# One written-out program order for all engines in a fused attention and MLP kernel, with the MLP weights loaded ahead of the second group

## Chip, cores, metric

The kernel runs on one core of a Trainium2 chip. The metric is device time in microseconds, the median of several executions. A "profile" below is one execution taken by the hardware profiler; its span runs from the first to the last instruction and is about 1.8 us shorter than the time of the same execution. Each execution lists the mean granted TensorE clock, and is called slow when it is over 1.5% above the fastest of the same kernel.

## The reference

```python
# q, k, v: (4, 8, 768, 64); lam: (8,); blocks of 64 positions
intra = einsum('bhic,bhjc->bhij', qb, kb) * Dmask            # lower triangle, lam ** distance
intra = einsum('bhij,bhjd->bhid', intra, vb)
inter = einsum('bhid,bhde->bhie', qb * lam_pow, kv_state)
out[block] = intra + inter
kv_state = lam ** 64 * kv_state + einsum('bhsd,bhse->bhde', kb * rev_pow, vb)
# then an MLP on the 3072 tokens, d_model 512, d_ff 2048
h = x @ w_in
g = h + sin(alpha * h) ** 2 / alpha
y = g @ w_out
```

Attention is cut into 24 *units* (half of the heads, 256 positions of one batch). Four units make one *group* of 512 tokens, so there are six groups. For each group the MLP has 16 *first-layer blocks* (four matmuls of 512 columns each, then sine on ScalarE, square on some engine, and a VectorE step) and four output tiles of 16 second-layer matmuls, taken in *second-layer blocks* of four.

## The kernel before

The program order is the order of execution of each engine. The old program writes it with loops: attention for groups 0 and 1 first (eight units, with filler matmuls that keep the TensorE clock up), then the first layer of group 0, and from group 2 on a regular pattern in which one attention unit stands between eight MLP blocks.

```python
def group(g, tag):                      # units 0 to 7
    for n in range(n0, n0 + 4):
        ...                             # scale q and k of unit n + 1
        if n >= WIN0 and n < WIN0 + WCH:
            load_w_in(n - WIN0)         # WIN0 = 5
        okv = new_okv()
        if n > 0:
            intermm(n - 1, okv); outmm(n - 1, okv)
        scores(n); domask(n); kvmm(n, okv); kv_copy(n, okv); kv_decay(n, 0)
        ...
        if nxt:
            transposes(n + 1, tag, True)
        busy(NB)                        # NB = 4 filler matmuls

def slot(n, out=True):                  # units 8 to 23: one row on TensorE
    okv = new_okv()                     # one PSUM tile for outputs of n - 1 and k*v of n
    if out: intermm(n - 1, okv)
    if n < NU: scores(n)
    if out: outmm(n - 1, okv)
    if n < NU: kvmm(n, okv)
    ...                                 # copies, masks, kv update

for n in range(12, NU + 8):             # the steady part
    at = {0: [L(slot, n), ...], 1: [L(dec, ...), L(scale_k, n + 2, G), L(cast_v, n + 2, G)]}
    macro(at, "21212121" if n % 4 == 0 else ... "12121212")   # 1: first layer, 2: second layer
```

Squares in the steady part are on VectorE, scalings, v casts and kv updates on POOL, PSUM copies on ScalarE.

## Time and profile before

227.76 us median of 3 runs (226.99 to 228.04). The page of the old kernel: busy time of engines, then forty slices of the span, 5.7 us each; a digit is the busy share in tenths, and for PEclk the granted clock.

```profile
span 227.1 us, 5244 instructions
...
PE 207.8 (91%) x2054; PEld 108.9 (48%) x2077; DVE 158.3 (70%) x268; ACT 115.7 (51%) x200; POOL 114.0 (50%) x176
...
PE   8777679997997779999999999999999999999993
...
PEclk9996999999999969999999999999999999999999
DMA  5999599999769999984877777484233022201424
```

TensorE is the limit from about 85 us on (slice 15, counted from 0). Before that, slices with 6 and 7 show it waiting. Its timeline (start, duration, engine, source line, operation, output and inputs, form, count, and in brackets the idle time before and what ended it) shows the first MLP matmuls at 33.23 us (three records of this group are missing, so the true first one can lie 0.2 us earlier):

```profile
32.66 0.42 PE L320 MATMUL okv<-ST,VB 64*64 64x128 bf16 x16
33.23 2.97 PE L349 MATMUL hps<-xt,w_in_sb 128*128 128x512 bf16 x13 [0.16 <-issue]
```

In the steady part a unit is one row of matmuls between two MLP blocks. The same timeline around 101 us:

```profile
100.57 1.03 PE L377 MATMUL ops<-w_out_sb,gall 128*128 128x512 bf16 x4
101.43 0.22 PE L305 MATMUL okv<-QT,kvbd_1801 128*128 128x128 bf16 x1
...
101.75 0.42 PE L226 MATMUL sp<-QT 64*64 64x128 bf16 x16
102.00 0.39 PE L320 MATMUL okv<-ST,VB 64*64 64x128 bf16 x16
102.22 0.29 PE L254 MATMUL okv<-VB,KD 64*64 64x64 bf16 x16
102.45 1.04 PE L349 MATMUL hps<-xt,w_in_sb 128*128 128x512 bf16 x3
```

The unit begins at 101.43 and the next MLP block at 102.45: about 1.0 us for it. Durations overlap, so starts are what one reads here.

**A ledger.** I price TensorE's useful work by its undisturbed durations in this trace (a four-matmul MLP block 0.865 us, transposes of one q or k 0.22, scores 0.25, outputs 0.25 and 0.075 for each matmul with a kv state, k*v 0.25 or, from unit 16 on, 0.125), and call *lost* the start of an instruction minus the work before it. The old kernel has lost about 22 us at its first MLP matmul. "At the first block of group 1" is read for it at the same amount of work (25.1 us), as its order differs: 48.1 us, so 23.0 lost. At the end of TensorE's work (222.9 us) it has lost 30.2; a tail of 4.2 us follows, to store the last tile. The ledger is good to about 0.3 us.

### The profile page before, as it was taken

The page shows a single profiled execution, that of the slowest core. Times are in us where ns is not written, and L with a number is a line of the kernel's source. Part 1 is how long each engine was busy: PE and PEld are TensorE (multiplying, and loading weights), DVE is VectorE, ACT ScalarE, POOL GpSimd, SP SyncE. Part 2 cuts the span into 40 slices and gives each one's busy share as a digit, 9 for nine tenths or more (in the row PEclk, how much of TensorE's full clock was granted, in tenths as well). Part 3 has the DMA queues.
Part 4 walks back from the last instruction along what each step waited for, and adds up shares of the span by engine and source line. Part 5 has one row for each costly group of instructions (what it writes and reads, how often), then busy time and mean ns, then how long its engine had stood idle before and what let it go on. Part 6 is the DMA issues. An engine that isn't in the chain of part 4 may idle for free.

```text
span 227.1 us, 5244 instructions
## 1 busy us (share of the span) xinstructions
PE 207.8 (91%) x2054; PEld 108.9 (48%) x2077; DVE 158.3 (70%) x268; ACT 115.7 (51%) x200; POOL 114.0 (50%) x176
## 2 busy tenths in 40 slices
PE   8777679997997779999999999999999999999993
PEld 5465444433444345554554555455455444444452
DVE  3866756988895486798887998867987747667000
ACT  2463659964645345645554554445455535554121
POOL 5665995275635459999999855742611000000000
PEclk9996999999999969999999999999999999999999
DMA  5999599999769999984877777484233022201424
GB/s 149 293 289 274 139 177 185 216 213 168 227 166 171 243 204 299 200 207 95 210 158 173 153 190 180 102 208 62 56 73 68 0 49 46 46 9 40 92 49 92
DMA packets 63849, 33.92 MB, mean 149 GB/s; under 512 B 19648, under 2 KB 60880, under 8 KB 63824
## 3 DMA queue, kind: packets, MB, share of 16 engines
q1 hardware_dynamic: 59488, 29.31, 56.7%
q0 software_dynamic: 4224, 4.19, 11.4%
q8 instruction: 16, 0.26, 0.5%
q10 hardware_dynamic: 112, 0.07, 0.1%
q14 instruction: 9, 0.07, 0.1%
HBM read 27.28 MB, written 6.29 MB: 148 GB/s over the span
## 4 chain that ended last, share of the span: by engine, by line
PE 67%; DMA 11%; SPq 6%; DVE 5%; POOL 4%; issue 2%; ACT 2%; ACTq 0%; POOLq 0%
PE ops L377 32%; PE hps L349 26%; DMA st_v<-in_v_dram 8%; SPq L80 5%; DMA st_k<-in_k_dram 3%; PE sp L226 2%; DVE gall L363 2%; PE okv L320 2%; PE okv L305 2%; POOL KD L169 2%; SPq L209 1%; PE okv L254 1%; DVE QL L160 1%; PE bz L427 1%; PE pt L196 1%
## 5 line engine op out<-in xcount | busy, mean ns | idle before, releaser
L349 PE MATMUL hps<-xt,w_in_sb 128*128 128x512 bf16 x370 | 94.3, 379 | 2.4 <-DVE gall L363 1.5
L377 PE MATMUL ops<-w_out_sb,gall 128*128 128x512 bf16 (+1 forms) x391 | 94.7, 372 | 1.1 <-issue 0.7
L377 PEld LDWEIGHTS <-gall 128*128 128x128 bf16 x400 | 38.7, 98 | 42.9 <-issue 0.5
L349 PEld LDWEIGHTS <-w_in_sb 128*128 128x128 bf16 x384 | 36.8, 98 | 45.8 <-issue 3.0
L169 POOL TENSOR_TENSOR KD<-st_k,R 128x512 bf16<-128x512 f32 x24 | 27.5, 1144 | 13.0 <-DMA st_k<-in_k_dram 8.9
L237 DVE TENSOR_TENSOR ST<-sp,mask 128x512 bf16<-128x512 f32 x48 | 30.8, 683 | 3.3 <-PE sp L226 3.1
L384 ACT COPY ob<-ops 128x512 f32<-128x512 f32 (+1 forms) x25 | 14.2, 569 | 16.3 <-PE ops L377 16.3
L331 ACT CAST xt<-okv 128x512 bf16<-128x512 f32 x24 | 14.1, 586 | 6.7 <-PE okv L254 5.8
L178 ACT CAST VB<-st_v 128x512 bf16<-128x512 f32 x14 | 8.7, 623 | 14.8 <-DMA st_v<-in_v_dram 14.8
L160 POOL TENSOR_TENSOR QL<-st_q,E 128x512 bf16<-128x512 f32 x12 | 12.8, 1070 | 0.0
L427 PE MATMUL bz<-zeros 128*128 128x256 bf16 x60 | 10.6, 332 | 1.1 <-DVE warm L94 1.1
L226 PE MATMUL sp<-QT 64*64 64x128 bf16 x384 | 10.4, 228 | 1.2 <-ACT QT L200 0.7
L160 DVE TENSOR_TENSOR QL<-st_q,E 128x512 bf16<-128x512 f32 x12 | 8.7, 728 | 2.2 <-DMA st_q<-in_q_dram 2.1
L320 PE MATMUL okv<-ST,VB 64*64 64x128 bf16 x384 | 10.2, 226 | 0.0
L226 PEld LDWEIGHTS <-QT 64*64 64x64 bf16 x384 | 6.8, 111 | 3.6 <-issue 0.9
L427 PEld LDWEIGHTS <-zeros 128*128 128x128 bf16 x60 | 6.7, 119 | 2.7 <-DVE warm L94 1.1
L254 PE MATMUL okv<-VB,KD 64*64 64x64 bf16 x320 | 7.4, 198 | 0.1
L320 PEld LDWEIGHTS <-VB 64*64 64x64 bf16 x384 | 7.0, 111 | 1.0 <-issue 0.2
L180 POOL CAST VB<-st_v 128x512 bf16<-128x512 f32 x10 | 6.8, 683 | 0.0
L200 ACT COPY QT<-pt 128x512 bf16<-128x512 bf16 x8 | 4.7, 590 | 3.8 <-issue 1.7
L254 PEld LDWEIGHTS <-KD 64*64 64x64 bf16 x320 | 6.2, 114 | 0.4 <-issue 0.2
L196 PE MATMUL pt<-iden,KD 128*128 128x128 bf16 x32 | 3.4, 232 | 2.9 <-POOL KD L169 2.8
(530 smaller groups left out, 303.7 us busy)
## 6 DMA issues: line engine op xcount, KB each, us to landing
st_q<-in_q_dram SPq DMA_DIRECT2D x24, 256.0 KB, 3.6
st_k<-in_k_dram SPq DMA_DIRECT2D x24, 256.0 KB, 4.1
st_v<-in_v_dram SPq DMA_DIRECT2D x24, 256.0 KB, 4.4
out_dram<-ob SPq DMA_DIRECT2D x46, 128.0 KB, 2.5
w_in_sb<-in_moe_w_in_dram POOLq DMA_DIRECT2D x4, 512.0 KB, 6.6
w_out_sb<-in_moe_w_out_dram POOLq DMA_DIRECT2D x4, 512.0 KB, 15.3
QT<-QL SPq DMA_TRANSPOSE x16, 3.4
QT<-KD SPq DMA_TRANSPOSE x16, 2.6
```

The source lines that it names most:

```text
L80: ld = nc.sync.dma_start(out=tl[:].rearrange("p h two e -> p h (two e)"), in_=src[b, hh * HH:(hh + 1) * HH, tp * W:(tp + 1) * W, :] .rearr ...
L160: eng.tensor_tensor(out=QL[:], in0=stage[u][0][:].rearrange("p h two e -> p two h e"), in1=E[:, :, hs].unsqueeze(3).to_broadcast([P, 2, HH ...
L169: eng.tensor_tensor(out=KD[:], in0=stage[u][1][:].rearrange("p h two e -> p two h e"), in1=R[:, :, hs].unsqueeze(3).to_broadcast([P, 2, HH ...
L226: nc.tensor.matmul(out=sp[hd][half[c], par, hp, :], lhsT=QT[half[hd], 1, par, hp, half[c]], rhs=QT[half[hd], 0, :, hp, half[c]], start=Tru ...
L237: nc.vector.tensor_tensor(out=ST[:, hd], in0=sp[hd][:], in1=mask[:].unsqueeze(2).to_broadcast([P, 2, 2, P]), op=ALU.mult)
L254: nc.tensor.matmul(out=okv[half[hd], c, 2 * P + hp * D:2 * P + (hp + 1) * D], lhsT=KD[half[c], par, h, :], rhs=VB[half[c], par, h, :], sta ...
L320: nc.tensor.matmul(out=okv[half[hd], c, hp * P:(hp + 1) * P], lhsT=VB[half[c], par, 2 * hp + hd, :], rhs=ST[half[c], hd, par, hp, :], star ...
L331: nc.scalar.copy(out=xt[g][:, 2 * hh:2 * hh + 2, bb, :, :].rearrange("p hp c i -> p c hp i"), in_=okv[:, :, 0:2 * P].rearrange("p c (hp i) ...
L349: f1mm[g, f] = nc.tensor.matmul(out=hps, lhsT=w_in_sb[:, c, f * P:(f + 1) * P], rhs=xt[g][:, c].rearrange("p b c i -> p (b c i)"), start=( ...
L377: f2mm[:] = [nc.tensor.matmul(out=ops[:], lhsT=gall[g][:, f, m * P:(m + 1) * P], rhs=w_out_sb[:, f, col], start=(f == 0), stop=(f == NFC - ...
L384: nc.scalar.copy(out=ob[:], in_=ops[:])
L427: nc.tensor.matmul(out=bz[:], lhsT=zeros[:, :P], rhs=zeros[:], start=True, stop=True)
```

## The change

The intent: one explicit order of all steps on all engines, found offline on a model of engines and queues. The MLP is to start after group 0's attention alone, with w_in loaded before most of group 1's attention and w_out during the first layers of groups 0 and 1, so that TensorE is useful earlier. The loops are replaced by a list; a token is step.unit:engine(:PSUM bank), as `k.15:T` for k*v of unit 15 on TensorE, `sqr.1.10:V` for a square on VectorE, `wi.2:G` for chunk 2 of w_in issued by POOL.

```diff
+ORDER = """
+ld.0.0:S ld.0.1:S sk.0:V sq.0:G tq.0:T:3 tk.0:T:0 ld.0.2:S ...
+tq.1:T:3 tcq.1:V tk.1:T:2 tq.2:T:1 tck.1:V s.1:T m.1.0:V m.1.1:V tq.3:T:0 cv.3:A tcq.2:A o.0:T
+tk.2:T:3 tck.2:A tk.3:T:2 a.1.0:V n.1.0:G s.2:T sq.4:V sk.4:V x.0.0:A o.1:T tck.3:V ...
+...
+sk.6:V f1.0.0:T tk.5:T:3 f1a.0.1:T:2 f1.0.1:T f1a.0.2:T:4 f1.0.2:T wi.1:G m.4.1:V n.1.1:G k.5:T
+sin.0.0:A sin.0.1:A sin.0.2:A sqr.0.0:V f1a.0.3:T:5 f1.0.3:T kc.5:A tck.5:V sqr.0.1:G wi.2:G cv.6:V
+k.6:T sqr.0.2:A sin.0.3:A tk.6:T:0 stt.0.0:V wi.3:G sq.7:V ...
+...                                  # steady part: the pieces of a unit stand apart
+m.13.1:V k.15:T f2.1.0.3:T a.13.0:V kc.15:A oc.1.0:A s.14:T o.13:T sq.16:G sin.2.10:A cv.16:A
+x.13.0:A f2.1.1.0:T:3 a.14.0:V m.14.0:V tdq.16:S st.0.1.0:S st.0.1.1:S sq.17:G sq.18:G tdq.17:S
+...
+"""
-    NB = 4
-    for u in range(8):
-        load(u)
+    NKV, NQL, NQT, NST = 5, 4, 4, 3          # a little more buffering
...
-    def slot(n, out=True):
-        okv = new_okv()
+    def kvmm(u, **_):
+        okv[u] = ps.tile([P, 2, 512], FP32, name="okv", tag="okv", bufs=1)   # and the same in outmm
...
+    for item in ORDER.split():
+        name, eng, *bank = item.split(":")
+        kind, *ix = name.split(".")
+        DO[kind](*map(int, ix), eng=ENG[eng], bank=int(bank[0]) if bank else None)
```

The first four blocks of groups 0 and 1 are split into two halves (`f1a` and `f1`), so that a group may begin when half of its attention is ready. The arithmetic is unchanged; the filler matmuls between units go.

## The prediction

> From about 84 us on TensorE is the limit: busy 9.8 to 10.0 in each stretch of ten us, and the chain of waits is an unbroken row of four-matmul blocks of 0.86 us. A full round there (eight blocks plus one attention unit) takes 7.93 us, so a unit costs 7.93 - 8x0.864 = 1.0 us. All TensorE work is then 768 MLP matmuls x 0.216 = 166 us, 24 units = 24 us, transposes of eight units about 3.6 us: 194 us. The last matmul ends near 223.2, the store 3.9 us later. So the 84 us before the steady state hold nearly all the lost time: the timeline has the first MLP matmul only at 33.2 us, when 11-12 us of real work are done (21-22 us lost), and from there to the end 190 us pass for 182.6 us of work (7.4 us lost: group 0 paced by ScalarE/VectorE, then the 14.7 us in the chain for the st_v load of unit 8 behind w_out, POOL scaling, and one clock dip at 80-84 us).
>
> What the change does. Arithmetic stays; 32 filler matmuls go. Work moves between engines: by operations times traced durations DVE stays near 158 us, ScalarE rises from 116 to about 128, POOL falls slightly to 111. None exceeds TensorE's 194. The MLP starts after four units instead of eight (7 us of TensorE work), and w_in goes ahead of the loads of group two.
>
> Where the new start falls. Loads move at about 290 GB/s in the trace's packet records, one of 256 KB per 0.9 us. POOL issues w_in chunk 0 after casting v of unit 4, about 17 us. The Trainium skill, "DMA: Bandwidth & Descriptors" (Queues, rings and completion order), says the engines round-robin between queues packet by packet; this trace agrees: while w_out and loads shared the engines, w_out wrote 143 GB/s (286 read) and the loads got 72. So a w_in chunk needs about 3.7 us, landing near 22.5, and the loads crawl. In TensorE's order the transpose of q of unit 6 stands before the first MLP matmul and waits for the 19th load and POOL's 1.1 us scaling: start about 24 us, against 33.2. If no gap followed, the end would be 24 - 7 + 194 + 4 = 215 us.
>
> Gaps expected: q of unit 7 is scaled by POOL behind w_in chunks 2 and 3, themselves behind a square: 2-3 us at about 28-32 us. Without fillers the clock halves at times before and at the MLP start (this trace already dips for 3.4 us at 18.8 despite them): about 1 us. Group 0 and 1 are ScalarE-limited (32 us against 28 on TensorE up to the first second-layer matmul), partly hidden: 1-2 us. In units 8 to 11 and group 2 POOL and DVE are as full as TensorE: about 1 us. Sum about 4 (to 9). Prediction 219 us, range 214 to 224.5; faster by over 2% 0.8, within 2% 0.17, slower 0.03.
>
> Right if: first MLP matmul at 22-26 us; no TensorE loss after about 85 us; same 3.9 us tail; second-layer start about 54-58 us; granted clock lower before 30 us; ScalarE busy about 128 us.
>
> Wrong if: one late landing stalls all engines' strict orders; loads starve behind w_in longer than 4 us a chunk; DVE squares beside POOL stretch (0.42 to 1.2 us now) and pace group 2; or the order hides even the early gaps (then below 215).

## The result

The changed kernel takes 242.2 us median of 4 runs (239.75 to 243.52) against 227.38 us (226.55 to 228.04) for the old one on the same chip. Ratios are the mean time of one kernel's fast runs over the mean of the other's fast runs of the same rounds, so not quite the ratio of the medians: 1.053, with a 95% interval of 1.043 to 1.063. It is slower; 219.0 was predicted.

Two of the four runs, the profiled one among them, are slow (243.5 us; the fast ones are 239.75 and 240.9). The profile of the changed kernel is therefore read for what happens where, and sizes are taken from the experiments, most of whose profiles are of fast runs.

The page after:

```profile
span 241.7 us, 5272 instructions
...
PE 216.5 (90%) x2049; PEld 112.1 (46%) x2077; DVE 166.2 (69%) x290; ACT 119.1 (49%) x207; POOL 110.3 (46%) x148
...
PE   8487599699959999998999997999999999999990
...
PEclk9955569799979999999999999999999999999998
DMA  5999979990898999984863994404811200305314
```

The start is earlier and the clock is at half from 11 to 35 us (this is what the Trainium skill, "TensorE: Matmul & The Clock Gate", Part 1, says of an idle TensorE: it falls to a 4/8 clock and needs sustained work to come back; the trace agrees in that PEclk reads 5 there). But PE is "9", not full, in the later slices too. What TensorE waited for, in total, times and longest (us):

```profile
PE hps L452 <- DMA w_in_sb<-in_moe_w_in_dram: 3.7, 2, 1.9
PE hps L452 <- DVE gall L486: 2.9, 1, 2.9
...
PE ops L495 <- DVE gall L486: 1.3, 1, 1.3
```

The two waits for w_in in TensorE's timeline are the first MLP matmul, and block 8 of group 0, which needs chunk 2:

```profile
29.14 1.89 PE L452 MATMUL hps<-xt,w_in_sb 128*128 128x256 bf16 x8 [1.90 <-DMA w_in_sb<-in_moe_w_in_dram]
...
44.72 1.54 PE L452 MATMUL hps<-xt,w_in_sb 128*128 128x512 bf16 x4 [1.82 <-DMA w_in_sb<-in_moe_w_in_dram]
```

POOL's timeline says why chunk 2 was late. Chunks 2 and 3 stand in POOL's order behind a square (the row with output s), which waited 7.54 us for ScalarE's sine, and that for the first MLP block:

```profile
24.21 0.80 POOL L253 DMA_DIRECT2D w_in_sb<-in_moe_w_in_dram  x1
25.79 0.62 POOL L405 TENSOR_TENSOR kvs<-kvx,LHP 128x128 f32<-128x128 f32 x1 [0.78 <-DVE kvx L393]
33.96 1.07 POOL L481 TENSOR_TENSOR s<-s 128x512 bf16<-128x512 bf16 x1 [7.54 <-ACT s L472]
34.98 1.54 POOL L253 DMA_DIRECT2D w_in_sb<-in_moe_w_in_dram  x2
```

The chunks were issued at 34.98 and chunk 2 was used at 44.72, over 9 us later; the median from issue to landing was 9.6 us, against 6.6 in the old kernel.

The wait of 2.9 us on VectorE, at 69.6 us, comes from one square there and from what POOL did meanwhile. VectorE, then POOL:

```profile
64.05 3.98 DVE L481 TENSOR_TENSOR s<-s 128x512 bf16<-128x512 bf16 x1
67.95 0.28 DVE L405 TENSOR_TENSOR kvs<-kvx,LHP 128x128 f32<-128x128 f32 x1
```

```profile
63.87 0.80 POOL L261 DMA_DIRECT2D w_out_sb<-in_moe_w_out_dram  x1
64.69 1.05 POOL L276 TENSOR_TENSOR KD<-st_k,R 128x512 bf16<-128x512 f32 x1
65.70 2.04 POOL L276 TENSOR_TENSOR QL<-st_q,E 128x512 bf16<-128x512 f32 x2
```

The square takes 0.42 us in the median of this trace, here 3.98, and ends at 68.03, just after POOL's row of three scalings (67.74). The Trainium skill, "SBUF — State Buffer", section "SBUF: two separate sides", says that a VectorE operation with two SBUF inputs and a POOL operation that reads SBUF share one port pair under an exclusive lock, and the loser blocks. The square is such an operation. Its recorded start, however, is 0.64 us before that of the first scaling, while POOL was issuing a chunk of w_out; why it didn't finish in that time, the trace doesn't show.

The steady part after, for the same stretch of a unit's pieces:

```profile
132.53 0.42 PE L344 MATMUL sp<-QT 64*64 64x128 bf16 x16
132.88 0.40 PE L420 MATMUL okv<-QT,kvbd 128*128 128x128 bf16 x4
133.20 0.42 PE L429 MATMUL okv<-ST,VB 64*64 64x128 bf16 x16
133.55 1.90 PE L452 MATMUL hps<-xt,w_in_sb 128*128 128x512 bf16 x7
...
138.84 0.31 PE L375 MATMUL okv<-VB,KD 64*64 64x64 bf16 x8
```

Scores and outputs alone took 133.55 - 132.53 = 1.02 us of TensorE, and k*v comes later, by itself. At the end, the stores. Old kernel (ACT copies of the two halves of the last tile, and the last store's issue), then the changed one:

```profile
223.28 0.37 ACT L384 COPY ob<-ops 128x256 f32<-128x256 f32 x1 [1.37 <-PE ops L377]
223.68 0.55 ACTq L389 DMA_DIRECT2D out_dram<-ob  x1
```

```profile
236.24 0.37 ACT L267 COPY ob<-ops 128x256 f32<-128x256 f32 x1 [1.33 <-PE ops L518]
236.64 0.56 ACTq L528 DMA_DIRECT2D out_dram<-ob  x1
236.79 0.53 SPq L528 DMA_DIRECT2D out_dram<-ob  x1
237.36 1.40 SPq L510 DMA_DIRECT2D out_dram<-ob  x2
```

In the changed kernel two stores of earlier tiles (L510) are issued last, up to 238.8 us. The tail, from TensorE's end to the span's end, is 5.7 us instead of 4.2.

The ledger, in us lost by stage (e2, e3, e11 are experiments told below; each column sums):

| stage | before | after (slow run) | e3 (fast run, front as after) | e2 | e11 |
|---|---|---|---|---|---|
| up to the first block of group 1 | 23.0 | 30.0 | 26.6 | 23.1 | 23.0 |
| from there to the last block of group 1 | 6.4 | 5.8 | 3.8 | 4.3 | 4.2 |
| from there to TensorE's end | 0.8 | 7.5 | 6.9 | 7.2 | 6.0 |
| lost in all | 30.2 | 43.3 | 37.3 | 34.6 | 33.2 |
| tail | 4.2 | 5.7 | 5.7 | 5.6 | 4.1 |

So after minus before in these profiles is 7.0 - 0.6 + 6.7 + 1.5 = 14.6 us, which is 241.7 - 227.1. The front's part is 3.6 us in e3, a fast run with the same front. At the first MLP matmul both kernels have lost about 22 us: the changed one starts four microseconds earlier, with four microseconds less work done. In the old kernel's own profile, about 2 us of the 6.4 fall into a stretch at half clock from 80 to 84 us (the 6 in its PEclk row).

### The profile page after: what moved, and what is told of

The parts are those of the page before. It is cut to its first block, busy times and chain, and to the rows that moved or that the text cites. A ratio compares the mean times of both kernels' runs of the same rounds, so it can differ in the third digit from the quotient of the medians.

```text
span 241.7 us, 5272 instructions
## 1 busy us (share of the span) xinstructions
PE 216.5 (90%) x2049; PEld 112.1 (46%) x2077; DVE 166.2 (69%) x290; ACT 119.1 (49%) x207; POOL 110.3 (46%) x148
## 4 chain that ended last, share of the span: by engine, by line
PE 65%; DVE 9%; DMA 7%; issue 6%; ACT 4%; SPq 4%; POOL 2%; ACTq 0%; POOLq 0%
PE ops L495 31%; PE hps L452 25%; SPq L243 4%; DMA w_in_sb<-in_moe_w_in_dram 4%; DMA st_k<-in_k_dram 3%; ACT s L472 2%; DVE gall L486 2%; PE sp L344 2%; DVE s L481 2%; PE okv L429 2%; PE okv L420 2%; PE okv L375 1%; PE ops L518 1%; DVE ST L354 1%; DVE kvbd L397 1%
## 5 line engine op out<-in xcount | busy, mean ns | idle before, releaser
L452 PE MATMUL hps<-xt,w_in_sb 128*128 128x512 bf16 (+1 forms) x403 | 94.4, 379 | 7.4 <-DMA w_in_sb<-in_moe_w_in_dram 3.7
L472 ACT ACTIVATE s<-hps,alpha_sb 128x512 bf16<-128x512 f32 x96 | 64.9, 688 | 59.5 <-PE hps L452 50.5
L495 PE MATMUL ops<-w_out_sb,gall 128*128 128x512 bf16 x353 | 84.7, 381 | 2.8 <-DVE gall L486 1.3
L486 DVE SCALAR_TENSOR_TENSOR gall<-s,r_sb,hps 128x512 bf16<-128x512 bf16 x96 | 69.6, 742 | 22.7 <-POOL s L481 12.4
L481 POOL TENSOR_TENSOR s<-s 128x512 bf16<-128x512 bf16 x25 | 26.3, 1054 | 81.5 <-ACT s L472 72.1
L495 PEld LDWEIGHTS <-gall 128*128 128x128 bf16 x368 | 34.9, 98 | 42.9 <-issue 2.4
L481 DVE TENSOR_TENSOR s<-s 128x512 bf16<-128x512 bf16 x33 | 20.5, 621 | 11.0 <-ACT s L472 10.9
L479 ACT ACTIVATE s<-s 128x512 bf16<-128x512 bf16 x38 | 23.6, 630 | 0.9 <-DVE gall L486 0.3
L276 POOL TENSOR_TENSOR QL<-st_q,E 128x512 bf16<-128x512 f32 x19 | 20.4, 1075 | 4.2 <-DMA st_q<-in_q_dram 3.8
L267 ACT COPY ob<-ops 128x512 f32<-128x512 f32 (+1 forms) x16 | 8.9, 557 | 24.8 <-PE ops L495 22.3
L267 ACT CAST xt<-okv 128x512 bf16<-128x512 f32 (+1 forms) x18 | 10.4, 577 | 14.1 <-PE okv L429 14.1
L397 DVE TENSOR_TENSOR kvbd<-kvx,LBD 128x256 bf16<-128x256 f32 x17 | 11.4, 669 | 0.6
```

The lines of the kernel that those rows point to most:

```text
L267: nc.scalar.copy(out=out, in_=in_)
L276: eng.tensor_tensor(out=t[:], in0=stage[u, j][:].rearrange("p h two e -> p two h e"), in1=tab[:, :, hh * HH:(hh + 1) * HH].unsqueeze(3).to ...
L452: mlp[0] = nc.tensor.matmul(out=hps[g, f][:].rearrange("p (b i) -> p b i", b=2)[:, bs] .rearrange("p b i -> p (b i)"), lhsT=w_in_sb[:, c, ...
L472: nc.scalar.activation(out=s1[g, f][:], in_=hps[g, f][:], func=ACTF.Sin, scale=alpha_sb[:, f:f + 1])
L479: nc.scalar.activation(out=s2[g, f][:], in_=x[:], func=ACTF.Square)
L481: eng.tensor_tensor(out=s2[g, f][:], in0=x[:], in1=x[:], op=ALU.mult)
```

## The experiments

Fifteen kernels ran; all gave correct outputs. The theories: **A**, the half clock after the fillers went; **B**, late w_in chunks; **C**, VectorE work starved beside POOL; **D**, the order of the steady part; **E**, the order of the last stores; **G**, the early order of units 0 to 3, which delays the start.

### e1: fillers put back

```diff
# in the changed kernel, after each transpose pair, k*v and output step ahead of the first MLP matmul
+        for _ in range(8):
+            nc.tensor.matmul(out=unused_columns, lhsT=zeros[:, :P], rhs=zeros[:, :P], start=True, stop=True)
```

> The changed kernel with 8 filler matmuls (128 columns each, into unused PSUM columns) after each transpose, k*v and output step that stands before the first MLP matmul; nothing else moves. Theory A (the lost fillers leave the TensorE clock at half from 11 to 35 us, and this slows the early chain and the first MLP blocks): clock near 1.0 from about 10 us on, first MLP matmul no later than 29 us, 5 to 8 us faster than the changed kernel (about 232 to 236). Rival B (the loss comes from late w_in chunks and from squares on DVE beside POOL, the cold clock is only a symptom of waiting): under 3 us gain, the waits at 44.7 us for w_in and at 69.6 us for DVE stay as long as now.

Measured: 237.3, 238.7 and 240.6 us in the fast runs, at a mean clock of 0.99, ratio 1.049. The gain on the changed kernel's 1.053 is within the interval, though the clock was full. A is not the main cause. The fillers take TensorE time themselves, so this run shows that putting them back doesn't pay, not what the clock alone is worth. The profiled run was a freak: 1226.92 us, with

```profile
PE 1217.1 (99%) x2245; PEld 388.0 (32%) x2245; DVE 155.3 (13%) x290; ACT 123.9 (10%) x207; POOL 107.4 (9%) x148
```

every matmul some six times too long from start to end. No change of the clock is recorded in its trace, so that its mean clock reads 1.000. It tells nothing of the change.

### e2: chunks 2 and 3 of w_in behind chunk 1

```diff
-... wi.1:G m.4.1:V ... sqr.0.1:G wi.2:G ... stt.0.0:V wi.3:G ...
+... wi.1:G wi.2:G wi.3:G m.4.1:V ... sqr.0.1:G ... stt.0.0:V ...
```

> The changed kernel with w_in chunks 2 and 3 issued directly behind chunk 1 in POOL's order, ahead of the square they stand behind now. Theory B1 (the late w_in chunks cost a wait and a clock dip): the wait for w_in at 44.7 us (1.8 us) and the half clock at 45 to 48 us go, 2 to 5 us faster. Rival A: the loads of units 6 and 7 starve behind the weights for about 7 us more and the first-layer blocks after the fourth wait for transposes of unit 7 instead; no gain or slower.

Measured: 235.68 us median (234.82 to 236.83), ratio 1.036. The wait at block 8 is gone; the first MLP matmul is at 27.6 us. Against the changed kernel's 1.053 that is about 1.8% or 4 us. B is confirmed as a part; the steady part still loses 7.2 us in the ledger, and most later kernels are built on this one.

### e3: squares of groups 1 to 3 from VectorE to ScalarE

```diff
-sqr.1.2:V ... sqr.1.10:V ... sqr.3.11:V
+sqr.1.2:A ... sqr.1.10:A ... sqr.3.11:A        # all squares of groups 1 to 3 that VectorE had
```

> The changed kernel with all squares of groups 1, 2 and 3 that DVE does given to ScalarE at the same places of the order. Theory C (DVE's squares starve while POOL works: one took 4.0 us at 64 us against 0.42 alone, and TensorE then waits 2.9 us and falls to half clock for 3.4 us): that wait and that dip go, DVE busy falls by 10 us or more, 3 to 7 us faster. Rival: the order is bound by early TensorE time, ScalarE becomes the pacing engine in group 1; within 2 us of the changed kernel.

Measured: 238.08 us (237.71 to 239.14), ratio 1.047. The stall moved to the next operation of VectorE with two SBUF inputs. VectorE in e3, then POOL:

```profile
61.13 3.11 DVE L405 TENSOR_TENSOR kvs<-kvx,LHP 128x128 f32<-128x128 f32 x1
```

```profile
61.03 1.06 POOL L276 TENSOR_TENSOR KD<-st_k,R 128x512 bf16<-128x512 f32 x1
62.04 2.04 POOL L276 TENSOR_TENSOR QL<-st_q,E 128x512 bf16<-128x512 f32 x2
```

A kv update of 0.28 us took 3.11 and ended with POOL's row, and TensorE waited 2.3 us. This fits C's mechanism; moving the victim of it is no repair.

### e4: the old kernel without fillers

```diff
-    NB = 4
+    NB = 0
```

> The kernel before without the 4 filler matmuls per unit of its first eight units (the 28 at the start stay). Theory A (fillers keep the clock up): half clock through most of 10 to 36 us as in the changed kernel, first MLP matmul 1 to 3 us later, first MLP blocks at half rate; 3 to 6 us slower than before (about 230 to 233). Rival: the old order is bound by loads and POOL there, and the clock does not matter: within 1.5 us of before.

Measured: 228.8 us (228.17 to 229.62), ratio 1.005 (0.997 to 1.013), although its clock was at half from 18.4 to 35.5 us:

```profile
PEclk9996558999999999999999999999999999999999
```

So 17 us at half clock cost the old kernel 0.5%, or 1.2 us, and by the interval between nothing and 3 us; TensorE's priced work in these 17 us is only about 7 us, so the slower matmuls mostly filled what would have been waits. In the profile the span is that of the old kernel, 227.1 us. A's 3 to 6 us are not there.

### e5: e2 with the fillers

```diff
+ both edits, that of e1 and that of e2
```

> All four runs of this call start from the second experiment's kernel (w_in chunks 2 and 3 early: 235.7 us, profiled span 233.0). This one adds the filler matmuls of the first experiment, whose profile was lost to an outlier. Theory A' (the cold clock costs only the half-rate stretch of the first MLP blocks, 27.6 to 30 us, about 1 us, since the early chain waits for loads): clock near 1.0 from 10 us on, first MLP matmul at 26 to 28 us as now, 0 to 2 us faster. Rival (the cold clock slows the chain of the first units): first MLP matmul 3 us earlier and 4 us or more faster.

Measured: 237.63 us (236.76 to 238.22), ratio 1.039. The clock was full from the start to 63.5 us, and the first MLP matmul came at 29.4 us, later than in e2. The clock doesn't set the start, and A, as the account of the whole loss, is refuted. The half clock is not free, though; what it costs is under "The clock" below.

### e6: e2, squares of groups 1 to 3 on ScalarE and later kv updates on POOL

```diff
-sqr.1.2:V ... a.8.0:V ... n.3.1:V ... a.13.0:V ...
+sqr.1.2:A ... a.8.0:G ... n.3.1:G ... a.13.0:G ...     # a and n from group 1 on
```

> From the second experiment's kernel: squares of groups 1 to 3 from DVE to ScalarE as in the third, and from group 1 on all kv-state updates from DVE to POOL, so that DVE runs almost no instruction with two SBUF inputs beside POOL. Theory C' (any such DVE instruction starves while POOL runs its scalings back to back; in the third experiment the victim was just the next one, a kv update of 3.1 us against 0.28): the stall of 2.9 us of TensorE at 62.7 us goes, no DVE instruction over 1.5 us after 45 us, 2.5 to 5 us faster (about 231 to 233). Rival: POOL, now longer by some 20 us of work, becomes the pacing engine for units 8 to 15 and nothing is won.

Measured: 235.38 us (233.13 to 237.04), ratio 1.028. TensorE's wait on VectorE at 65 us is gone, and a wait on POOL is in its place:

```profile
63.53 0.43 PE L375 MATMUL okv<-VB,KD 64*64 64x64 bf16 x16 [2.16 <-POOL KD L276]
```

From block 8 of group 2 to the end, e6 loses 4.4 us where e2 loses 7.1 (32.9 - 28.5 and 34.6 - 27.5): there the repair works. In the whole time the gain on e2 is not clear of the noise (intervals 1.019 to 1.036 and 1.028 to 1.043).

### e7: e2 with three stores ahead of the last tile's

```diff
-lt.0:T:1 ltc.0:A st.5.2.0:S lt.1:T:3 ltc.1:A st.5.1.1:S st.5.2.1:S
+st.5.1.1:S st.5.2.0:S st.5.2.1:S lt.0:T:1 ltc.0:A lt.1:T:3 ltc.1:A
```

> From the second experiment's kernel: the last three whole-tile stores (group 5, tiles 1 and 2) stand before the last tile's stores in SyncE's queue instead of behind them; nothing else. Theory E (the order of the stores costs the end: 5.6 us from the last matmul to the end against 4.2 in the kernel before): tail back to about 4.2 us, 1.0 to 1.6 us faster. Rival: the tail is the last tile's own copy and store, no change.

Measured: 234.45 us (233.18 to 237.06), ratio 1.025; the tail is 232.7 - 228.6 = 4.1 us against e2's 5.6. E is confirmed in the trace, 1.5 us; the gain in the whole time alone isn't clear of the noise.

### e8: e2 with five units in one row again

```diff
+    def slot(n, **_):                    # k*v of n, scores of n, outputs of n - 1: one row, one PSUM tile
+        okv[n - 1] = okv[n] = ps.tile([P, 2, 512], FP32, name="okv", tag="okv", bufs=1)
+        outmm(n - 1, lambda: scores(n), False)
+        kvmm(n, False)
-k.13:T ... o.12:T ... s.13:T        # likewise 14, 15, 16, 23
+slot.13:T
```

> From the second experiment's kernel: the scattered pieces (scores, k*v, output) of units 13, 14, 15, 16 and 23 put back together in one row on TensorE, as in the kernel before, with one PSUM tile. Theory D (every break between MLP blocks and attention pieces costs TensorE: a unit in one row takes 1.01 us beyond its MLP neighbours, one in pieces 1.25 to 1.46): these five units take about 1.01 us each, the unstalled sum of their pieces falls by about 1.7 us, 1 to 2.5 us faster. Rival: the pieces were scattered for a reason, the rows now wait for masks and kv states and lose as much.

Measured: 237.43 us (236.44 to 240.59), ratio 1.038, so no gain. In its profile, of a slow run, the row of unit 23 took 1.01 us as in the old kernel, those of 13 to 16 took 1.16, 2.61, 1.52 and 2.05, because a row begins only when the last of its inputs is there, and the other engines' order was made for pieces: TensorE waited 1.42 us for VectorE's kv state at 106.56. Rows alone, in an order made for pieces, give nothing. D stays open with this run.

### e9: e2 with units 0 to 3 one after another

```diff
-tq.1 tk.1 tq.2 s.1 tq.3 o.0 tk.2 tk.3 s.2 o.1 k.2 k.3 tq.4 s.3 tq.5 k.4 tk.4 o.2 o.3 s.4 tq.6 f1a.0.0   # TensorE
+tq.1 tk.1 o.0 s.1 k.1 tq.2 tk.2 o.1 s.2 k.2 tq.3 tk.3 o.2 s.3 k.3 o.3 f1a.0.0 f1.0.0 tq.4 tk.4 ...
+# wi.0 on POOL right behind the scaling of k of unit 3
```

> The e2 kernel (w_in chunks 2 and 3 early) with units 0 to 3 taken one after the other as the old kernel does (each unit's scalings, transposes, scores, masks and outputs before the next unit's transposes), with w_in chunk 0 issued by POOL right behind the scaling of k of unit 3 (about 15 us instead of 19.3), and with all work on units 4 to 6 except their loads behind the first MLP block; from then on e2's order. Theory G (the breadth-first early order, in which the outputs of units 1 to 3 stand behind scalings and transposes of units 4 to 6 and so behind later loads, is why the early MLP start brought nothing): outputs of unit 3 before 20 us instead of 25.6, first MLP matmul at 22 to 24 us instead of 27.6, TensorE's lost time there 16 to 18 us instead of 20.4, and if the rest keeps pace a total 2 to 4 us under e2's, ratio to before 1.02 to 1.03. Rival (the loads and w_in share the DMA engines and that alone sets when units 4 to 7 are there): the first MLP matmul comes earlier, but the time is lost again within group 0, in waits for loads of units 4 to 7 or for w_in chunks, and the total stays within 1 us of e2's, ratio about 1.035.

Measured: 244.07 us (243.13 to 244.93), ratio 1.069. The outputs of unit 3 were at 20.8 us and the first MLP matmul at 23.7 us, with 18.3 us lost there, as G says, and yet the kernel is far slower. The first fault in its trace is an order of my own: on POOL a kv update stood ahead of chunks 1 to 3 and waited.

```profile
29.48 0.40 POOL L405 TENSOR_TENSOR kvs<-kva,LHP 128x128 f32<-128x128 f32 x1 [7.15 <-DVE kva L269]
...
30.82 2.29 POOL L253 DMA_DIRECT2D w_in_sb<-in_moe_w_in_dram  x3
```

The three chunks were issued at 30.8 instead of 24 us: the fault of the changed kernel again, and TensorE then waited 1.25 us for chunk 1 at 39 us. Waits are only half of what was lost in group 0; see "The clock" below.

### e10: e9 with the loads of unit 4 on held until chunk 0 has landed

```diff
+        if (u, j) == (4, 0):
+            after(loads[u, j], w_in[0])
```

> As e9, but the load of q of unit 4 (and with it all later loads of that queue) is held until w_in chunk 0 has landed, so that chunk 0 does not share the DMA engines with loads. Theory G with a share of the DMA: chunk 0 lands about 5 to 6 us after its issue instead of 8 to 9, first MLP matmul at 20 to 21 us; the loads of units 4 to 7 then come 4 to 5 us later, so the wait for them moves into group 0 (unit 4's transposes wait at about 24 us for 1 to 3 us) and the total is within 1.5 us of e9's either way. If the DMA engines' total work up to the last load of unit 7 (24 loads of 0.9 us and four chunks of 3.6 us when alone, so about 38 us) sets the pace of group 0, both kernels reach the end of group 0 (first block of group 1) with the same lost time within 1 us, that of e2 or a little less.

Measured: 246.11 us (243.7 to 246.46), ratio 1.074. The first MLP matmul is at 21.9 us without a wait for w_in, so chunk 0 does land sooner when it shares with nothing. Then VectorE waits 4.1 us and POOL 6.3 us for the loads that were held. TensorE waited 2.9 us for a later chunk at 41.7 us. What one stream gets the other lacks.

### e11: e2 up to the end of group 1, then the old kernel's order

```diff
# e2's list is cut before k.12; from there the tokens of the old loops, with slot() as in e8
+slot.12:T x.11.0:A m.12.0:V m.12.1:V kc.12:A a.12.0:G n.12.0:G tdk.13:S f2.1.0.0:T:3 sk.14:G cv.14:G f1.2.0:T:1
+sin.2.0:A sqr.2.0:V stt.2.0:V f2.1.0.1:T f1.2.1:T:2 ...
```

> A hybrid: the e2 kernel (new order with early w_in) up to its last block of group 1, and from the unit 12 on, where the second-layer blocks of group 1 begin, exactly the old kernel's order: each attention unit in one row on TensorE with its outputs and k*v in one PSUM tile, squares on VectorE, scalings, v casts and kv updates on POOL, copies on ScalarE, old order of stores at the end. At that point e2 has lost 27.4 us of TensorE time against the old kernel's 29.4. Theory D (what the new order loses after about 83 us, 7.2 us in e2 against 0.8 in the old kernel, comes from its own fine order there: units in pieces, elementwise work moved about): the loss after 83 us falls to 1 to 2 us, TensorE ends at about 222 us, the tail is 4.2 us as in the old kernel, and the time is equal to before's or up to 1.5% less: ratio 0.985 to 1.005. Rival (the early part of the new order leaves debts, late loads, full rings or late kv updates, that make the later stalls, or the clock does): the hybrid still loses 4 us or more after 83 us and stays at 1.02 or above.

Measured: 232.56 us median (230.76 to 237.11; fast runs to 233.32), ratio 1.017 (1.011 to 1.024). TensorE waited 4.4 us at the seam, where the two orders meet, for DMA transposes of units 12 and 13, and the ledger rises there from 27.2 to 31.9. Behind it, from 97 us to the end, it rises only to 33.2: 1.3 us lost in 129 us, of which about 0.5 at one wait for an output copy by ScalarE (192 us). Its timeline in the steady part:

```profile
126.68 1.03 PE L461 MATMUL hps<-xt,w_in_sb 128*128 128x512 bf16 x4
127.55 0.39 PE L427 MATMUL okv<-QT,kvbd 128*128 128x128 bf16 x4
127.86 0.42 PE L343 MATMUL sp<-QT 64*64 64x128 bf16 x16
128.11 0.39 PE L438 MATMUL okv<-ST,VB 64*64 64x128 bf16 x16
128.33 0.29 PE L375 MATMUL okv<-VB,KD 64*64 64x64 bf16 x8
128.56 1.04 PE L461 MATMUL hps<-xt,w_in_sb 128*128 128x512 bf16 x3
```

That is 1.01 us a unit, as in the old kernel. D is confirmed: the front is e2's, and the loss behind the seam is nearly the old kernel's. What was put back is the whole of the old steady part, that is rows, shared PSUM tile, engines of the elementwise work and order of stores; which of these matters most, this run doesn't say.

### e12: e6 and e7 together

```diff
+ both edits, that of e6 and that of e7, on top of e2
```

> The two small repairs of e6 (squares of groups 1 to 3 on ScalarE, kv updates on POOL from group 1 on) and e7 (three stores ahead of those of the last tile) together, on top of e2. If their gains add, as they concern different stretches: e2's ratio 1.0356 less 0.008 and less 0.011, so about 1.017 (1.01 to 1.023), profiled span near 230 us, TensorE end near 225.7 and a tail of 4.1 us. It stays slower than before, because the pieces of units remain. If it is below 1.005, the pieces cost less than the traces say; if above 1.025, the gains of e6 or e7 were noise.

Measured: 234.1 us (232.93 to 235.07), ratio 1.026 (1.021 to 1.030), above what was expected. Both repairs are in the trace: a tail of 232.3 - 228.3 = 4.0 us, and 4.4 us lost from block 8 of group 2 to the end. But the front, which is e2's token for token, had lost 26.1 us at the first block of group 1 instead of e2's 23.1, with the first MLP matmul at 28.9 us behind a wait of 1.4 us for w_in. The same front lost 22.8 to 23.5 us in the profiles of e2, e6, e7 and e11, and 26.0 to 26.2 in those of e8, e12 and e13. Which of the two it is turns on when chunk 0 lands: the start is 1.3 us later in e12 than in e2, and the clock then stays at half until 34.9 us instead of 30.0. Why chunk 0 lands late in some executions is not settled.

### e13: as e11, with the seam eight blocks later

```diff
-# list cut before k.12
+# list cut before f1.2.8; from there the old order as far as its steps are not done yet
+s.12:T m.12.0:V m.12.1:V a.12.0:G n.12.0:G f2.1.0.0:T:3 ... slot.13:T ...
```

> As e11, but the seam between the two orders is later: e2's order up to and with the first eight first-layer blocks of group 2 (where e2 has lost 27.5 us), then the old kernel's order. In e11 TensorE waited 2.5 and 2.0 us at the seam for the DMA transposes of units 12 and 13, and lost only 0.8 us in all the 129 us behind it. If those waits belong to the seam alone (theory D), they go: loss at the end 28 to 29.5 us instead of 32.7, TensorE end at 221 to 222.5 us, span 225 to 227 us, ratio to before 0.985 to 1.005. Rival (the debt is in the early part: the old order run from there always has to wait 4 to 5 us once for work that the new order's front has put off): a wait of the same size appears somewhere in the first 30 us behind the new seam and the ratio stays at 1.01 or above.

Measured: 235.5 us (232.61 to 237.04), ratio 1.029. The profiled run is slow, and its front had lost 26.2 us. TensorE waited again at the seam, 2.17 us put down to an earlier store's DMA and 0.45 on VectorE, and 4.7 us were lost there in all up to 104 us, in part at half clock (99.6 to 103.0 us). From 110 us to the end it lost 1.4 us. So D holds a second time, and the rival on the seam could not be excluded: a wait of some size sat at both seams. Whether it is a debt of the front or an artefact of splicing two orders stays open.

### e14: e9 repaired

```diff
+... wi.0:G wi.1:G wi.2:G wi.3:G ...       # all four behind the scaling of k of unit 3
+... f1.0.1 s.4 k.4 tq.5 f1a.0.2 f1.0.2 tk.5 k.5 f1a.0.3 f1.0.3 f1.0.4 f1.0.5 tq.6 o.4 s.5 f1.0.6 k.6 tk.6 f1.0.7 ...   # TensorE
```

> e9 was spoilt by my own order: I had put the kv update of unit 4 on POOL ahead of w_in chunks 1 to 3, POOL waited 7.2 us for it, and the chunks were issued at 30.8 us. Here, on top of e2: units 0 to 3 one after the other as in e9, all four w_in chunks issued in one go behind the scaling of k of unit 3 (about 15 us), and the work on units 4 to 7 moved behind the first-layer blocks in the order in which their loads can land while sharing the DMA engines. Theory G (the early start that was predicted can be had and kept, it needs the right early order): first MLP matmul at 22 to 24.5 us, first block of group 1 at 44.5 to 47 us with 19 to 22 us lost there (e2: 48.2 us, 23.1 lost), total 1.5 to 4 us under e2's, ratio 1.018 to 1.03. Rival (24 loads and the four chunks need about 38 us of the DMA engines, so what starts early waits later): 23 us lost or more at the first block of group 1, ratio 1.033 or above.

Measured: 246.05 us (244.89 to 247.08), ratio 1.076. First MLP matmul at 24.3 us, 18.9 us lost; at the first block of group 1, 32.4 lost. Behind a wait of 2.3 us for chunk 0 at the start, the main waits were for scalings and casts that stood too late in VectorE's order. TensorE:

```profile
32.08 0.61 PE L303 MATMUL pt<-iden,QL 128*128 128x128 bf16 x4 [2.90 <-DVE QL L276]
```

That scaling of q of unit 5 stood behind the masks and kv update of unit 4, and no wait of VectorE for a load is in the trace from 15 to 48 us. So the rival, which put the loss down to the loads, isn't shown by this run either: what failed is the hand-made order, and the half clock that went with it (see "The clock" below).

### e15: e14's front with e11's steady part

```diff
+ e14's list up to k.12, then the old order as in e11
```

> e14's front with e11's change to the old order from unit 12 on. If the gains add: ratio of e11 (1.017) less what e14 gains on e2 (0.7 to 1.7%), so 1.00 to 1.01, and under 1.0 only if the waits at the seam (4.9 us in e11) shrink too. Rival (what the front gains is lost at the next wait that does not depend on it): 1.017 as e11.

Measured: 240.94 us (239.56 to 243.07), ratio 1.053. The front lost 32.0 us up to group 1; the seam took 4.0 (37.7 to 41.7); from 107 us to the end it lost 1.4. The old steady part behaves the same behind both fronts.

No version of the new order beat the old kernel. The best, e11, is 1.7% above it.

## Why the prediction was wrong, point by point

The prediction's sum was 24 - 7 + 194 + 4 = 215, plus 4 us of gaps. The total work (194; the ledger gives 192.8) was right. Three terms were not: in e3's profile the loss at the start is 20.3 us instead of 24 - 7 = 17, the gaps are 17.0 instead of 4, and the tail is 5.7 instead of 4.

**"Gaps expected ... Sum about 4 (to 9)" is the step that failed.** From the first MLP matmul to TensorE's end the fast run e3 lost 37.3 - 20.3 = 17.0 us, and the slow profile of the changed kernel 43.3 - 22.3 = 21.0. (The prediction's own list of gaps adds up to 5 to 7 us, not 4.) e3's 17.0 are 6.3 up to the first block of group 1, 3.8 in group 1 and 6.9 behind it. Above all the prediction expected "no TensorE loss after about 85 us", as in the old kernel. There the loss is 6.9 to 7.5 us against 0.8. It took over the old kernel's price of a unit, 1.0 us, for an order that takes units apart. The trace of e2 prices the pieces between MLP blocks: k*v alone 0.34, scores with k*v 0.56, outputs with scores 0.89, scores with outputs 1.12, outputs alone 0.67. From unit 13 on, TensorE leaves the MLP 12 times in the old kernel, 11.96 us in all, and 23 times in e2, 18.2 us, of which one more set of scores (0.25) is no loss. Three of the 23 are longer than the same pieces elsewhere, by 2.7 us in all, the greatest through the wait of 1.31 us for VectorE's gall; the remaining 3.4 us is what the pieces cost. e6 and e12 agree: with VectorE's waits taken away 4.4 us are left. The three hybrids show that the order of the steady part as a whole makes the loss (1.3 to 1.4 us left in each behind the seam), with the reserve that each lost 4 to 5 us at its seam. That 3.4 us belong to the pieces themselves is read from the traces; e8, the one run that tried rows without the rest of the old order, gave nothing.

**"Start about 24 us" was wrong by 3 to 5 us.** It was 29.1 in the slow profile, 27.0 to 27.6 in the fast profiles of e2, e3, e6, e7 and e11, and 28.9 in that of e12. The outputs of units 1 to 3 stand behind transposes and scalings of units 4 to 6 in the order, and so behind later loads. e9 and e14, with the units one after another, started at 23.7 and 24.3: that part of G is right. But the prediction made the start worth its full difference, and those two runs show that it isn't: both were slower in total. An early start is kept only if everything behind it is ready in the order in which it is asked for. Whether some order can keep it stays open; the attempts e9, e10 and e14 failed, each through waits that I had made and through the half clock.

**"2-3 us at about 28-32 us" for the POOL work behind w_in was the right place and the wrong victim.** It was seen that chunks 2 and 3 stand behind a square; the wait was expected at q of unit 7, and came at block 8 of group 0, for chunk 2 itself. The chunk was priced at 3.7 us, from the sharing seen while w_out loaded. The DMA page of the Trainium skill ("DMA: Bandwidth & Descriptors", Queues, rings and completion order) says that queues take turns by packets, and the old trace's shares (143 and 72 GB/s in the prediction) fit that; but from issue to landing the chunks' median was 9.6 us in this kernel. Issued early (e2), they cost about 4 us less in total, half of it the wait (1.8 us) and half the stretch at half clock behind it.

**"same 3.9 us tail"**: it became 5.7 us where the ledger had 4.2, from the order of three stores; e7 gives 1.5 us back.

**The clock** was granted lower before 30 us, as the prediction said, but its price, "about 1 us", holds only for e2, e6 and e11. The same sixteen matmuls of group 0 (four half-blocks), at half clock in the changed kernel and at full clock in e6:

```profile
31.24 3.62 PE L452 MATMUL hps<-xt,w_in_sb 128*128 128x256 bf16 x16
```

```profile
29.48 1.91 PE L452 MATMUL hps<-xt,w_in_sb 128*128 128x256 bf16 x16
```

Price the work that TensorE begins at half clock between the first MLP matmul and the first block of group 1, and set it beside what is lost there. In the profiles with e2's front (e5's with fillers in it) the loss is that work plus 1.2 to 1.4 us, every time: e5 0 and 1.4, e6 1.0 and 2.4, e2 1.3 and 2.6, e11 1.4 and 2.7, e7 2.3 and 3.5, e8 and e13 2.8 and 4.1, e12 3.1 and 4.2. In e3 it is 3.3 of 6.6, in the changed kernel's slow profile 4.7 of 8.0, in e9 5.6 of 12.0 and in e14 7.1 of 13.8. So the half clock costs where there is work to do, and it makes about half of what the early starts of e9 and e14 lose again in group 0. The fillers took it away in e5, and e5 was no faster: its first MLP matmul came 1.9 us later than e2's, and a stretch at half clock came at 63 us instead. Whether a cheaper way to keep the clock up would pay wasn't tried.

**"DVE squares beside POOL stretch"** was named among the ways to be wrong. It happened, to 3.98 us, once at a place where TensorE waited 2.9 us for it. The ledger's second stage shows that it didn't decide the case: from the first to the last block of group 1 the new order loses less (5.8, in fast runs 3.8 to 4.3) than the old one (6.4), which has stalls of its own there.

Of the prediction's other marks, POOL was right (110.3 us busy, 111 predicted); ScalarE was busy 119.1 us (128), VectorE 166.2 (158), and the second layer began at 64.8 us in the slow profile and 61.4 in e3 (54 to 58).

In sum, the 12 to 13 us of the fast runs come from the steady part's order (6 to 7 us in the ledger), late weights (about 4, e2, with the half clock behind them) and the last stores (1.5, e7). These sizes are from different runs, so their sum is no exact account.

## What to carry to other kernels

Before changing an order, find what the old one's regular part already loses; here it was 0.8 us in 140, and little could be won there, while the order that takes its units apart lost six to seven more. In a fixed order each engine waits for its head: put DMA issues ahead of anything that depends on the data of a later stage, and keep operations that share a port or wait long out of their way. An earlier start is worth only what the stages behind it can take up, so check the lost time at the next stage boundary, not the first matmul, and see at which clock the early work ran.

## What the Trainium skill lacked or had wrong

- "SBUF — State Buffer" (SBUF: two separate sides) has the exclusive lock between POOL and VectorE operations with two SBUF inputs, held "for the whole instruction". It doesn't say that a VectorE operation can wait through a whole row of back-to-back POOL instructions: here a 0.42 us square took 3.98 us beside a DMA issue and three scalings, and in e3 a 0.28 us update took 3.11.
- "TensorE: Matmul & The Clock Gate" has the half clock, and among its terms a penalty of the throttled time times the missing share of the clock. That is too much for a kernel that waits meanwhile: 17 us at half clock would be 8.5 us by it and cost 0.5% (e4; 95% interval -0.3% to 1.3%), while what counted in the fronts of e2 to e13 was the work begun at half clock (see "The clock" above). It warns of unreliable clock events, but doesn't have e1's freak: one execution of 1226.92 us, all matmuls some six times too long, with no clock event, while the other three took 237 to 241 us.
- "TensorEngine Tiling (Array Packing)" (Tiling Modes) has it that a change of the tiling mode drains TensorE, but no page prices small 64x64 matmuls put between large ones by how they are grouped: 1.01 us for a whole unit in a row, 1.23 to 1.46 us for the same unit in pieces (k*v alone 0.34 and outputs with scores 0.89; or k*v alone 0.34 and scores with outputs 1.12). The 0.34 is the same for 16 matmuls (unit 14) and for 8 (unit 16).
- "DMA: Bandwidth & Descriptors" has the packet round-robin between queues. Here a 512 KB chunk of w_in took a median of 6.6 us from issue to landing in the old kernel and 9.6 us in the changed one, beside loads of 256 KB; the page doesn't give the time that a queued transfer takes to land when the queues share.
